# The output projection in Strassen's form, two blocks of tokens at once, in a fused Fourier-mixing and SoLU kernel

## The chip, the cores and the metric

The kernel runs on one core of a Trainium2 chip. The metric is the device time of one execution in microseconds; a time below is the median of three or four executions unless it says otherwise (of seven for the kernel before where it ran beside a batch). The engines are PE (TensorE, matmuls), PEld (its weight loads), DVE (VectorE), ACT (ScalarE), POOL (GpSimd) and SP (SyncE, which here only issues DMAs; "SPq" is its queue).

## The reference

```python
def _attn_ref(x, filt_r, filt_i):                  # x: 8 x 3136 x 256, float32
    X = np.fft.rfft(x, axis=1)
    Y = X * (filt_r + 1j * filt_i)[None, :, :]
    return np.fft.irfft(Y, n=x.shape[1], axis=1)   # then seen as 25088 x 256

def _moe_ref(x, w_in, w_out, g_ln):                # w_in 256 x 1024, w_out 1024 x 256
    h = x @ w_in
    e = np.exp(h - np.max(h, axis=-1, keepdims=True))
    solu = h * (e / (np.sum(e, axis=-1, keepdims=True) + 1e-09))
    mu = np.mean(solu, axis=-1, keepdims=True)
    var = np.mean((solu - mu) ** 2, axis=-1, keepdims=True)
    return (solu - mu) / np.sqrt(var + 1e-06) * g_ln @ w_out
```

## The kernel before

The 25088 tokens are 196 blocks of 128. The main loop has one `step` per block, 196 steps and some to drain. An even and an odd step are a pair; the hidden layer of a pair (`x @ w_in`) is already in Strassen's form, seven products instead of eight. The Fourier transforms of later batch entries are spread over the same steps as small jobs: `pa` (first stage forward), `pb` (second stage forward), `pc` (second stage back), `py` (first stage back). Their rows and tables come by DMA from SyncE's queue.

The projection takes the blocks one at a time. A block's `solu` is transposed in 32x32 pieces by VectorE, regrouped by four DMAs on SyncE's queue, and multiplied with eight chunks of `w_out`, 256 columns wide:

```python
def regroup(g, a):                       # one block a step
    turned = turns[g].rearrange("p (k q) b i -> p k q (b i)", q=4)
    solu_ts[g, a] = st = upool.tile([P, KF, P], FP32, ...)
    for q in range(4):
        nc.sync.dma_start(out=st[32 * q:32 * q + 32, :, :],
                          in_=turned[32 * a:32 * a + 32, :, q, :])
    if a == 0:                           # every fourth step: 1/sqrt(var + eps)
        ...                              # two small GpSimd instructions make rs
        for c in range(4):
            for i in range(4):           # 16 tiny copies put rs into row order
                nc.gpsimd.tensor_copy(out=rss[g][32 * i:32 * i + 32, c:c + 1],
                                      in_=rs[32 * c:32 * c + 32, i:i + 1])

def project(k, ps, half):
    ...
    for f in range(KF // 2 * half, KF // 2 * half + KF // 2):
        nc.tensor.matmul(out=ps, lhsT=solu_ts[divmod(k, 4)][:, f, :], rhs=w_out_sb[:, f, :],
                         start=(f == 0), stop=(f == KF - 1), skip_group_check=True)
```

Row buffers and lead of the loads (every x piece and every row piece of the way back passes through the pool "r"):

```python
for name, bufs in (("r", 4), ("t1", 2), ("t2", 3), ("p", 2), ("g", 2))
...
at = max(t - 3, row_loads[n - 4][0] if n >= 4 else -1)   # step at which a row load is issued
ahead(t, 3).append(lambda sp=sp, i=i: sp.fetch(i))       # t2: spectrum rows, three steps ahead
ahead(t, 2).append(lambda sp=sp, i=i: sp.fetch_de(i))    # de: their table, two steps ahead
```

Of the kernel before, what the change touches and what calls it, by code (L numbers as in the profile page):

```python
# [17 lines left out]
P = 128  # L18
# [14 lines left out]
LAG = 8  # L33
# [47 lines left out]
def kernel(  # L81
# [32 lines left out]

    w_in_sb = consts.tile([P, 7, DFF // 2], FP32, name="w_in_sb")
    w_out_sb = consts.tile([P, KF, C], FP32, name="w_out_sb")
    g_sb = consts.tile([P, KF], FP32, name="g_sb")
    neg_half = consts.tile([P, 4], FP32, name="neg_half")
    ones = consts.tile([P, P], FP32, name="ones")
    w_bar = consts.tile([P, C], FP32, name="w_bar")  # L120
# [3 lines left out]
    y = consts.tile([P, KD, PAIR], FP32, name="y")  # L124

# [19 lines left out]
    class Spectrum:  # L145
# [24 lines left out]
        def first(self, i, halves, ps, evac):  # L170

            if 0 in halves:
                self.t1s[i] = self.pools["t1"].tile([NK, NCH, C], FP32, name=f"t1_{self.n}_{i}",
                                                    tag="t1")
            for j, u in enumerate(halves):
                nc.tensor.matmul(out=ps[0:NK, j], lhsT=wf_t, rhs=self.xs[i][0:NR, 2 * u:2 * u + 2, :],  # L176
                                 start=True, stop=True)
            n0, n = 2 * halves[0], 2 * len(halves)
            evac(out=self.t1s[i][:, n0:n0 + n, :].rearrange("p n c -> p (n c)"),  # L179
                 in_=ps[0:NK].rearrange("p a b -> p (a b)"))  # L180

        def store_first(self, i, dmas):
            b, ch = divmod(i, NH // NCH)
            by_16(dmas, d1[self.n][b].rearrange("s (a n) c -> (s a) n c", a=4)[
                :, NCH * ch:NCH * ch + NCH, :], self.t1s.pop(i))
            del self.xs[i]
# [22 lines left out]
        def multiply(self, i):  # L209
# [5 lines left out]
            turned = self.pools["p"].tile([P, 2, C], FP32, name=f"i_{self.n}_{i}", tag="i")[:, 0:cols, :]  # L215
# [50 lines left out]
    with ExitStack() as st:  # L266
# [53 lines left out]
        for h in range(4):  # L320
            weights.append((w_out_sb[:, 2 * h:2 * h + 2, :].rearrange("p k d -> p (k d)"),
                            w_out_words[256 * h:256 * h + 256].rearrange("(k p) d w -> p k d w", p=P)))
# [13 lines left out]
        for i in range(2 * NH // NCH):  # L336
# [3 lines left out]
            sp.store_first(i, (nc.scalar.dma_start, nc.gpsimd.dma_start))  # L340
# [5 lines left out]
        w11, w21, w22, wt1, wt2, wt3, w12 = (w_in_sb[:, i, :] for i in range(7))  # L346
        for to, a, b in ((wt1, w12, w11), (wt3, w22, w12), (wt2, w22, wt1), (w12, w21, wt2)):
            nc.vector.tensor_tensor(out=to, in0=a, in1=b, op=ALU.subtract)
# [34 lines left out]
    def prepare_w_out(step):  # L383


        if step == 0:
            nc.vector.memset(ones, 1.0)
            for f in range(KF):
                nc.vector.tensor_scalar(out=w_out_sb[:, f, :], in0=w_out_sb[:, f, :],
                                        scalar1=g_sb[:, f:f + 1], scalar2=-float(DFF), op0=ALU.mult,  # L390
                                        op1=ALU.mult)
        elif step == 1:
            ps = psum("o", "ps_mean")[:, 0, :]
            for f in range(KF):
                nc.tensor.matmul(out=ps, lhsT=ones, rhs=w_out_sb[:, f, :],
                                 start=(f == 0), stop=(f == KF - 1))
            nc.scalar.mul(w_bar, ps, 1.0 / DFF)
        else:
            for f in range(KF):
                nc.vector.tensor_tensor(out=w_out_sb[:, f, :], in0=w_out_sb[:, f, :], in1=w_bar,  # L400
                                        op=ALU.subtract)


    ps_b = pool("ps_b", 1, PSUM)
    ps_o = pool("ps_o", 2, PSUM)
    ps_m = pool("ps_m", 1, PSUM)

# [304 lines left out]
```

## Time and profile before

| | before |
|---|---|
| median, range | 1795.54 us, 1795.15 to 1799.84 (3 runs) |
| PE busy | 96% of the span |
| first main-loop matmul | at 176.3 us |
| last pair of blocks begins | 49.2 us before the end |
| mean granted clock | 0.988 |

Two things are added here. The first is the view by stretches of time; the columns after the bounds are the length of the stretch, busy time of PE, PEld, DVE, ACT and POOL, then the granted PE clock, the DMA share and GB/s:

```profile
176.00:402.00 226.00, 206.14 (x726) 124.65 (x725) 126.89 (x266) 129.98 (x220) 113.01 (x242) 0.98 0.88 232
402.00:1746.00 1344.00, 1343.64 (x5094) 901.47 (x5093) 913.03 (x1899) 771.87 (x1272) 542.38 (x1335) 1.00 0.61 159
```

In the 1344 us of the second stretch PE has 0.4 us without work, and its clock is 1.00: it is not only busy, it runs at full speed. The second is VectorE's largest group (busy us and mean ns of one come before the second bar) and what SyncE's queue waits for (us in all, times, longest):

```profile
L512 DVE SCALAR_TENSOR_TENSOR h<-e,rsum,h 128x1024 f32<-128x1024 f32 x196 | 256.4, 1308 | 7.1 <-DMA x<-in_x_dram 0.3
```

**A measure used throughout.** I add the PE work of each pair at full clock (14 x 429 ns hidden, 6.91 us projection before and 6.22 after, 0.86 us per pa, pb and pc, 0.87 per py) and subtract it from the pair's length in the trace, start of product 1 to start of the next pair's product 1. I call the rest the **excess**. Before, the first ten pairs (steps 0 to 19) have 33.6 us of it and the other 87 intervals 7.1 us.

### The profile page before, as it was taken

Reading aid. Unit: us, or ns where it says so; the run is one execution under the profiler, and the core shown is the slowest. Engines: PE = TensorE matmul, PEld = TensorE weight load, DVE = VectorE, ACT = ScalarE, POOL = GpSimd, SP = SyncE. Lnnn points to the kernel's source line nnn. Section 1 sums busy time; section 2 is a strip of 40 time slices with the busy share of each in tenths; the row PEclk is TensorE's granted clock in tenths of the full one; section 3 lists DMA queues with packets and bytes.
Section 4 is the critical chain, followed back from the end, with each engine's and each line's share of the span. In section 5 each row is a group of like instructions: output and inputs, shape, how many; then the busy total and the mean of one; then the engine's idle time right before and its main releaser. Section 6 shows DMA issues by size and latency. Waiting matters only on the chain.

```text
span 1795.5 us, 22752 instructions
## 1 busy us (share of the span) xinstructions
PE 1721.1 (96%) x6324; PEld 1112.1 (62%) x6324; DVE 1155.9 (64%) x2370; ACT 990.9 (55%) x1623; POOL 718.8 (40%) x1698
## 2 busy tenths in 40 slices
PE   6589889999999999999999999999999999999998
PEld 2125455566666666766666666676777677666666
DVE  0794545567666665677777655667676766677773
ACT  2265555566666655566666555555655555555452
POOL 3242544465455543335445333344443332324331
PEclk9699999999999999999999999999999999999999
DMA  9786789987799765577667565567775444433334
GB/s 270 250 258 191 217 224 247 246 215 205 207 232 222 191 184 145 151 167 199 180 174 203 142 162 146 127 170 191 191 188 133 107 120 108 107 103 104 102 96 119
DMA packets 323180, 313.98 MB, mean 175 GB/s; under 512 B 26465, under 2 KB 284514, under 8 KB 323056
## 3 DMA queue, kind: packets, MB, share of 16 engines
q1 hardware_dynamic: 292496, 219.79, 48.3%
q0 software_dynamic: 28768, 86.45, 16.6%
q10 hardware_dynamic: 1792, 6.29, 1.0%
q8 instruction: 53, 0.87, 0.2%
q14 instruction: 71, 0.58, 0.1%
HBM read 131.55 MB, written 81.40 MB: 119 GB/s over the span
## 4 chain that ended last, share of the span: by engine, by line
PE 83%; DMA 9%; DVE 3%; ACT 2%; issue 1%; POOL 1%; SPq 1%; DVEq 0%; ACTq 0%; POOLq 0%
PE po L549 35%; PE m L464 30%; PE py L260 6%; PE pa L176 4%; PE pc L235 4%; PE pb L205 4%; DMA x<-in_x_dram 3%; DMA d<-t 2%; DMA t<-d 2%; DMA de<-de_tbl 1%; DVE p L226 1%; DVE p L224 1%; PE idle L370 1%; DMA solu_t<-turn 0%; DVE i L225 0%
## 5 line engine op out<-in xcount | busy, mean ns | idle before, releaser
L549 PE MATMUL po<-w_out_sb,solu_t 128*128 128x256 f32 x3136 | 724.5, 379 | 2.4 <-DMA solu_t<-turn 1.6
L549 PEld LDWEIGHTS po<-w_out_sb,solu_t 128*128 128x128 f32 x3136 | 593.3, 190 | 190.0 <-issue 114.9
L464 PE MATMUL m<-w_in_sb,sums 128*128 128x512 f32 x784 | 399.1, 600 | 7.5 <-ACT h L474 7.5
L514 ACT ACTIVATE e<-h,nmu 128x1024 f32<-128x1024 f32 x196 | 225.1, 1149 | 223.3 <-DVE h L512 219.5
L464 PE MATMUL m<-w_in_sb,y 128*128 128x512 f32 x588 | 286.8, 597 | 0.1
L474 ACT COPY h<-m 128x512 f32<-128x512 f32 x294 | 172.4, 586 | 176.6 <-PE m L464 162.9
L512 DVE SCALAR_TENSOR_TENSOR h<-e,rsum,h 128x1024 f32<-128x1024 f32 x196 | 256.4, 1308 | 7.1 <-DMA x<-in_x_dram 0.3
L488 DVE CUSTOM_DVE_ANT_0 h<-m,h 128x512 f32<-128x512 f32 x196 | 133.9, 683 | 173.3 <-ACT h L474 86.0
L243 POOL DMA_DIRECT2D d<-g x101 | 77.2, 764 | 416.0 <-ACT g L238 407.0
L522 DVE STREAM_TRANSPOSE turn<-h 128x1024 f32<-128x1024 f32 x196 | 242.2, 1236 | 0.4 <-DVE ot L558 0.3
L496 ACT ACTIVATE e<-h,nmax 128x1024 f32<-128x1024 f32 x196 | 225.8, 1152 | 0.1
L558 DVE TENSOR_SCALAR ot<-po,rs_t 128x256 f32<-128x256 f32 x196 | 94.3, 481 | 171.6 <-issue 84.9
L464 PEld LDWEIGHTS m<-w_in_sb,sums 128*128 128x128 f32 x784 | 141.3, 190 | 96.0 <-issue 72.6
L541 POOL COPY rs_t<-rs 32x1 f32<-32x1 f32 x784 | 181.6, 232 | 35.7
L464 PEld LDWEIGHTS m<-w_in_sb,y 128*128 128x128 f32 x588 | 109.7, 191 | 112.7 <-issue 92.5
L224 DVE TENSOR_TENSOR p<-pb,f 128x512 f32<-128x512 f32 (+1 forms) x101 | 69.1, 685 | 149.9 <-ACT i L217 147.5
L176 PE MATMUL pa<-x,wf_t 98*100 98x512 f32 x256 | 138.3, 649 | 25.8 <-DMA x<-in_x_dram 21.3
L260 PEld LDWEIGHTS py<-wi_t,t 100*128 100x128 f32 x1024 | 131.7, 192 | 50.1 <-issue 31.5
L263 ACT COPY y<-py 128x392 f32<-128x392 f32 x128 | 108.2, 846 | 85.8 <-PE py L260 84.8
L179 ACT COPY t<-pa 100x512 f32<-100x512 f32 (+1 forms) x112 | 71.8, 646 | 133.5 <-PE pa L176 109.9
L260 PE MATMUL py<-wi_t,t 100*128 100x98 f32 x1024 | 132.0, 273 | 2.6 <-DMA t<-d 1.6
L205 PE MATMUL pb<-t,de 128*128 128x512 f32 (+1 forms) x250 | 108.1, 532 | 19.4 <-DMA t<-d 11.5
(65 smaller groups left out, 1441.4 us busy)
## 6 DMA issues: line engine op xcount, KB each, us to landing
solu_t<-turn SPq DMA_DIRECT2D x784, 128.0 KB
t<-d SPq DMA_DIRECT2D x99, 256.0 KB
d<-g POOLq DMA_DIRECT2D x99, 256.0 KB, 4.4
out_dram<-ot SPq DMA_DIRECT2D x196, 128.0 KB
x<-in_x_dram SPq DMA_DIRECT2D x64, 384.0 KB
t<-d SPq DMA_DIRECT2D x64, 384.0 KB
d<-t POOLq DMA_DIRECT2D x48, 384.0 KB, 5.8
f<-f_dram POOLq DMA_DIRECT2D x104, 128.0 KB, 5.7
```

Source lines behind the costliest of these rows:

```text
L176: nc.tensor.matmul(out=ps[0:NK, j], lhsT=wf_t, rhs=self.xs[i][0:NR, 2 * u:2 * u + 2, :], start=True, stop=True)
L205: nc.tensor.matmul(out=ps[:, w * j:w * j + w, :], lhsT=self.des[i][:, j, 0, :], rhs=t2[:, w * j:w * j + w, :], start=True, stop=True)
L260: nc.tensor.matmul(out=psv[:, i, :], lhsT=t4s[e, ch][:, i, cb * P:cb * P + P], rhs=wi_t, start=True, stop=True)
L464: nc.tensor.matmul(out=ms[j, bank], lhsT=lhsT, rhs=w_in_sb[:, w, :], start=m in (1, 2, 7), stop=True, skip_group_check=True)
L474: nc.scalar.copy(out=h_half(k, i), in_=ms[j, 0])
L488: nc.vector.tensor_tensor_reduce(out=h_half(k, i), in0=ms[j, bank], in1=h_half(*kept), scale=1.0, scalar=sofar, op0=ALU.add, op1=ALU.min, ...
L496: nc.scalar.activation(out=e, in_=hs[k], func=AFT.Exp, bias=nmaxs.pop(k)[:, 1:2], scale=-1.0, accum_out=esum)
L512: nc.vector.scalar_tensor_tensor(out=solu, in0=e, scalar=rsum, in1=solu, op0=ALU.mult, op1=ALU.mult, accum_out=nmu)
L514: nc.scalar.activation(out=e, in_=solu, func=AFT.Square, bias=nmu, scale=-float(DFF), accum_out=variances[g][:, i:i + 1])
L522: nc.vector.transpose(out=turns[g][:, :, i, :], in_=solus.pop(k).rearrange("p (f j) -> p f j", j=32))
L541: nc.gpsimd.tensor_copy(out=rss[g][32 * i:32 * i + 32, c:c + 1], in_=rs[32 * c:32 * c + 32, i:i + 1])
L549: nc.tensor.matmul(out=ps, lhsT=solu_ts[divmod(k, 4)][:, f, :], rhs=w_out_sb[:, f, :], start=(f == 0), stop=(f == KF - 1), skip_group_chec ...
```

## The change

Its intent: one more of the two large matrix products in Strassen's form. Two blocks of tokens and the two halves of `w_out`'s rows and columns make a 2x2 problem; seven chains of eight 128-column matmuls replace 32 of 256 columns. That costs four sums of `solu` (128x512) a pair, on GpSimd. The buffers for them come from the row buffers (4 to 3), from t2 (3 to 2) and from halved t1 tiles. GpSimd is relieved of the 16 small copies: the reciprocal roots now go through DRAM by DMAs on SyncE's queue.

```diff
-             for name, bufs in (("r", 4), ("t1", 2), ("t2", 3), ("p", 2), ("g", 2))}
+             for name, bufs in (("r", 3), ("t1", 3), ("t2", 2), ("p", 2), ("g", 2))}
...
+    def regroup(p):                                   # two blocks, in every even step
...
+        for i in range(2):
+            a = 2 * second + i
+            st = upool.tile([P, KF, P], FP32, name=f"solu_t_{p}_{i}", tag=f"solu_t{i}")
...
+            for q in range(4):
+                nc.sync.dma_start(out=st[32 * q:32 * q + 32, :, :],
+                                  in_=turned[32 * a:32 * a + 32, :, q, :])
...
+            rows = rs_dram.tile([P, 4], FP32, name=f"rows_{g}", tag="rows")
+            nc.sync.dma_start(out=rows, in_=rs)
             rss[g] = small.tile([P, 4], FP32, name=f"rs_t_{g}", tag="rs_t")
-            for c in range(4):
-                for i in range(4):
-                    nc.gpsimd.tensor_copy(out=rss[g][32 * i:32 * i + 32, c:c + 1],
-                                          in_=rs[32 * c:32 * c + 32, i:i + 1])
+            for b in range(4):
+                nc.sync.dma_start(out=rss[g][32 * b:32 * b + 32, :],
+                                  in_=rows.rearrange("(a p) b -> b p a", p=32)[b])
...
+    def project_sums(p, step):
...
+        if step == 0:
...
+            sum_of(s1, a21, a22, ALU.add)
+            sum_of(a21, a11, a21, ALU.subtract)
...
+        else:
...
+            sum_of(s2, s1, a11, ALU.subtract)
+            sum_of(s4, a12, s2, ALU.subtract)
...
+    def project(p, m):
...
+        for f in range(KF // 2):
+            nc.tensor.matmul(out=pos[p, bank], lhsT=lhs[:, f, :], rhs=w[:, f, :],
+                             start=f == 0 and m in (1, 2, 7), stop=True, skip_group_check=True)
...
-            ahead(t, 3).append(lambda sp=sp, i=i: sp.fetch(i))
+            ahead(t, 2).append(lambda sp=sp, i=i: sp.fetch(i))
```

The loads of a step's Fourier data stand at the end of the step, behind the regrouping, the roots and the output stores in SyncE's queue.

## The prediction

> **What bounds the kernel now.** I read the page's engine row and its forty slices first.
>
> ```profile
> PE 1721.1 (96%) x6324; PEld 1112.1 (62%) x6324; DVE 1155.9 (64%) x2370; ACT 990.9 (55%) x1623; POOL 718.8 (40%) x1698
> ...
> PE   6589889999999999999999999999999999999998
> ...
> DMA  9786789987799765577667565567775444433334
> ```
>
> The matrix engine (PE) is at 9 or more from slice 8 on; everything else has a quarter or more of its time free. A busy matmul engine can still be stretched by waits, so next came the waits of PE alone: from 401 to 1760 us they come to 0.3 us in all. From 176 to 401 us the longest are the two below; the rest of PE's 74 us without work lies before 176 us, in the first stage, which the change leaves alone.
>
> ```profile
> PE m L464 <- ACT h L474: 7.5, 5, 4.9
> PE pb L205 <- DMA de<-de_tbl: 4.6, 4, 2.0
> ```
>
> Then the groups, for what PE does and what one matmul costs:
>
> ```profile
> L549 PE MATMUL po<-w_out_sb,solu_t 128*128 128x256 f32 x3136 | 724.5, 379 | 2.4 <-DMA solu_t<-turn 1.6
> L464 PE MATMUL m<-w_in_sb,sums 128*128 128x512 f32 x784 | 399.1, 600 | 7.5 <-ACT h L474 7.5
> L260 PE MATMUL py<-wi_t,t 100*128 100x98 f32 x1024 | 132.0, 273 | 2.6 <-DMA t<-d 1.6
> L541 POOL COPY rs_t<-rs 32x1 f32<-32x1 f32 x784 | 181.6, 232 | 35.7
> ```
>
> The means (379, 600, 273) are latencies of overlapping instructions, so the cost must come from starts. The timeline of PE, in the quiet part and near 916 us:
>
> ```profile
> 1631.50 3.62 PE L549 MATMUL po<-w_out_sb,solu_t 128*128 128x256 f32 x16
> 1634.95 1.88 PE L464 MATMUL m<-w_in_sb,sums 128*128 128x512 f32 x4
> 1636.67 1.89 PE L549 MATMUL po<-w_out_sb,solu_t 128*128 128x256 f32 x8
> ...
> 1644.56 3.62 PE L549 MATMUL po<-w_out_sb,solu_t 128*128 128x256 f32 x16
> ```
>
> ```profile
> 916.15 1.03 PE L260 MATMUL py<-wi_t,t 100*128 100x98 f32 x8
> 917.02 1.05 PE L464 MATMUL m<-w_in_sb,sums 128*128 128x512 f32 x2
> ```
>
> Start to start: 3.45 us for 16 matmuls of 256 columns is 216 ns each; 1.72 us for 4 of 512 is 430 ns; 0.87 us for 8 of 98 is 109 ns. A pair of blocks repeats after 1644.56 - 1631.50 = 13.06 us, and that is its work: 14 x 429 ns (hidden layer, every fp32 product being two instructions) + 32 x 216 ns (projection) = 6.01 + 6.91 = 12.92. Adding the Fourier jobs (0.86 us for each pa, pb, pc; 0.87 for each py) to this I get the length of every pair from the 20th step on, within 0.2 us in nearly all and 0.4 in two. So for 88 of 98 pairs PE alone sets the time; the first ten pairs took 201 us for about 170 us of PE work, with the DMA engines 0.86 busy there.
>
> **What the Trainium skill says.** "TensorE: Matmul & The Clock Gate", section "Back-to-back issue gap", gives N/2.4 + 2.5 ns; section "LDWEIGHTS (loading the stationary operand)" gives columns/1.2, so 107 ns for 128 columns, whatever the rows. The trace has 429 and 216 ns for 512 and 256 columns: the first formula with twice the columns (429.2 and 215.8). For 98 columns that would be 84 ns. The single records show, in each chain of eight, 88, 110 and then 111 to 112 ns, and weight loads 112 ns apart: below about 130 columns the load sets the pace, 5 ns above the skill's 107. "GPSIMD Engine Reference", section "3.1 Elementwise — side-by-side cycle accounting", has 4497 ns for a two-input add of 2048 elements; the trace has a median of 457 ns for 128. A line through both gives 1.26 us for 512 (estimate). Its section "1. Specifications" says that GpSimd contends with VectorE instructions with two SBUF inputs: the trace agrees, the longest 128-element add took 1.53 us, about one 1.29 us SCALAR_TENSOR_TENSOR more.
>
> **The change part by part.**
> *Projection on PE.* Removed: 32 instructions a pair at 216 ns = 6.91 us. Added: 7 products x 4 chunks x 2 = 56 instructions of 128 columns. Streaming needs 256/2.4 + 2.5 = 109 ns, the weight load 112; the first two of a chain of eight stream (109), six follow the loads (112): 0.89 us a chain, 6.22 us a pair. So an eighth fewer multiplications become a tenth less time: 0.69 us a pair, 68 us in 98 pairs. This is all there is to win, and the 88 PE-bound pairs hold 60 us of it.
> *VectorE.* Out: 196 x 481 ns = 94 us. In: 4 x 98 pieces of 128 columns at some 0.33 us (481 less 128/0.96 ns; estimate) = 130 us. It stays near 80% of a shorter pair: quiet pair 10.3 of 12.4 us.
> *ScalarE.* 3 x 98 scaled copies of 128 columns, about 0.26 us each (586 ns at 512 columns less 384/1.2; estimate) = 78 us, to some 62%.
> *GpSimd.* Out: the 784 copies, 182 us. In: 4 x 98 sums of 512 elements, 1.26 us alone and perhaps 1.7 us beside VectorE: 490 to 670 us. It goes to 60 or 70%, up to 14 of 15.7 us in a pair with two Fourier units.
> *Order of sums.* The sums of a pair are asked for at the end of a 6 us step and used a step later (the step by odd and even halves is about 6 us each in the quiet part, 8 with Fourier jobs). The pair sums of the hidden layer now queue behind the first two on GpSimd, which wait for eight regrouping DMAs (0.65 us each on the queue; the last four only after the fourth product frees its buffer). Worked out: p4 ends 6.1 us into the even step, issues end at 9.0, land by 11.5, two sums to 14.5, the needed pair sum by 16; product 6 wants it at about 19. It holds, with some 3 us.
> *Queue of SyncE.* Every fourth step the reciprocal roots go through DRAM: one store, a wait for its landing (2 to 3 us, estimate from the 2.8 us of the page's quickest store), four small loads. The Fourier rows and tables behind them leave about 15.5 us after the step's start; they are now fetched two steps ahead (rows were three) and wanted at 18.3 us when the pair is 15.7 us. That is tight: I expect 0.5 to 2 us of PE waiting in about ten of the twenty such places, 10 us in all.
> *Fewer row buffers.* With three instead of four, loads only one step ahead go from 3 to 8, two steps ahead from 16 to 28 (of 104), nearly all before step 20. There too the half-size t1 buffers (three halves where there were two wholes) make ScalarE wait for a store in the five steps with two x pieces. I put 8 us on the first twenty steps, against 5 of the 7 us they could gain.
> *Drain.* At the end, the last pair's regrouping waits for the buffer two pairs back, then for sums: 3 us more.
> Sum: 1795.5 - 60 - 5 + 10 + 8 + 3 = 1751; rounded to 1750.
>
> **The rivals.**
> (1) *PE gains nothing because the weight load is the bound.* If a 128-column fp32 matmul with its own load took 123 ns, 56 of them would make 6.9 us, as before, and with GpSimd and the fetches on top the time would be 1800. Against it: loads 112 ns apart in 128 chains of eight, with the same 128 columns. If they overlapped fully (109 ns), 1740.
> (2) *GpSimd becomes the bound or delays product 6.* For: adds that wait a whole VectorE instruction, in-order stores in the same queue. Against: 3 us of slack at product 6 and some 2 us free in the fullest pair. If sums take 2.2 us, the Fourier pairs (about 40) lose 1 us each: 1780 to 1790.
> (3) *The fetches come late.* For: the longer SyncE queue, less lead, DMA engines at 0.84 to 0.86 until 636 us, with 31,000 more tiny packets. Against: 300 us from 1519 on have no Fourier unit and a DMA share of 0.4. If every pair before step 46 and in the two later Fourier stretches loses what it won, 1770.
> (4) *VectorE paces the Fourier pairs.* Its work there is 14.3 us, plus some 1.5 us waiting for ScalarE's turned copies: 15.8 against PE's 15.7. Worth under 5 us.
>
> **Range and chances.** The gain is capped by counting at 68 us (78 if loads hide wholly), so 1730 is nearly the floor. Losses of 10 to 20 us are likely, 40 possible, and a net loss would need two rivals at once. Predicted 1750, 8 in 10 within 1730 to 1778. The 2% line is 1759.6, inside the range: faster 0.66, within 2% 0.32, slower 0.02.
>
> **What would show it right or wrong.** Right: 5488 projection matmuls whose starts lie 111 to 112 ns apart, a quiet pair of 12.4 us where it was 13.06, GpSimd's new sums at 1.3 to 1.8 us, waits of PE on rows and tables (pb, pa, py) of 10 to 25 us in all, most before 500 us. Wrong in step one if the chain takes over 0.95 us or under 0.88. Wrong in the rest if PE waits for GpSimd at product 6 or at the summed products, if VectorE or ScalarE paces the quiet pairs, or if the first twenty steps grow by over 20 us.

## More of the kernel before

```profile
SPq L562 <- DVE ot L558: 589.1, 179, 8.5
```

SyncE's queue spends a third of the span holding a finished block's store until VectorE has made it. The loads stand behind that store in the queue, but they had lead enough: PE hardly waits for any of them after 401 us.

## The result, and the profile after

The changed kernel is correct and takes **1925.11 us** (1918.79 to 1933.53, four runs) against 1795.35 (four runs of the kernel before): ratio 1.072, 95% interval 1.0672 to 1.0768. The profiled run took 1931.8 us.

Engine row and two of the slice rows of the page, after:

```profile
PE 1724.5 (89%) x8692; PEld 1165.7 (60%) x8692; DVE 1235.1 (64%) x2586; ACT 1066.6 (55%) x1917; POOL 1091.5 (57%) x1306
...
PE   6679887888899999989989989989788999999996
...
PEclk8799888889999999999999999989989999999999
```

PE's busy time has not fallen although its work has, and its clock has digits of 7 and 8 where it had nines. The stretches say the same in numbers:

```profile
176.00:402.00 226.00, 184.92 (x713) 110.77 (x712) 109.78 (x244) 113.00 (x199) 113.34 (x161) 0.87 0.75 202
402.00:1760.00 1358.00, 1253.50 (x6733) 884.46 (x6732) 920.18 (x1935) 796.75 (x1451) 820.79 (x958) 0.97 0.58 154
```

In the long stretch PE is without work for 104 us of 1358 where it was for 0.4 of 1344, and it also runs at a granted clock of 0.97 instead of 1.00.

Yet the arithmetic of the matmuls came out. Timeline of PE in the quiet part, after (start, length of the group, line; L484 is the hidden layer, L595 the projection):

```profile
1744.74 1.02 PE L484 MATMUL m<-w_in_sb,y 128*128 128x512 f32 x2
...
1746.46 1.05 PE L595 MATMUL o<-w_out_sb,u 128*128 128x128 f32 x8
1747.35 1.06 PE L595 MATMUL o<-w_out_sb,solu_t 128*128 128x128 f32 x8
1748.24 1.88 PE L484 MATMUL m<-w_in_sb,s 128*128 128x512 f32 x4
...
1757.00 1.02 PE L484 MATMUL m<-w_in_sb,y 128*128 128x512 f32 x2
```

A chain of eight takes 0.89 us from start to start, 111 ns a matmul; the same product of the next pair comes 12.26 us later, where it was 13.06. The groups of GpSimd's sums and VectorE's largest, after:

```profile
L463 POOL TENSOR_TENSOR u<-solu_t 128x512 f32<-128x512 f32 x98 | 142.6, 1455 | 244.9 <-DMA solu_t<-turn 180.5
...
L532 DVE SCALAR_TENSOR_TENSOR h<-e,rsum,h 128x1024 f32<-128x1024 f32 x196 | 306.2, 1562 | 7.1 <-DVE rsum L529 0.3
```

The sum takes 1.46 us, inside the predicted 1.3 to 1.8. The SCALAR_TENSOR_TENSOR, which the change does not touch, went from 1308 to 1562 ns.

What PE waits for now (us in all, times, longest), and then SyncE's queue, both after:

```profile
PE pb L207 <- DMA de<-de_tbl: 78.2, 22, 8.5
PE pa L180 <- DMA x<-in_x_dram: 25.6, 13, 5.7
PE py L263 <- DMA t<-d: 22.5, 4, 12.3
```

```profile
SPq L555 <- PE o L595: 222.7, 79, 10.2
SPq L555 <- DVE turn L542: 202.0, 47, 9.0
SPq L566 <- DMA rows<-rs: 97.9, 49, 4.9
```

The wait for `de`, the table of a Fourier unit, was 4.9 us. It is the *last* load of its unit, so it stands for lateness of the queue. Of the 78.2 us, 70 are in 16 steps whose number divides by four, 4.4 us each. The queue has three holders now: L555, the regrouping, waits for the fourth product to free its buffer and for the transposes; L566, the loads of the roots, for the store before them to land, 49 times 2.0 us.

One case in full: the queue's work of step 62, which begins at 805.64 us on PE; its last two loads are for the Fourier unit of step 64, which begins at 819.69. SyncE's queue, after (start, length, line, what is issued):

```profile
806.52 8.10 SPq L555 DMA_DIRECT2D solu_t<-turn  x8
814.72 0.57 SPq L563 DMA_DIRECT2D rows<-rs  x1
816.93 1.84 SPq L566 DMA_DIRECT2D rs_t<-rows  x4
818.87 1.32 SPq L622 DMA_DIRECT2D out_dram<-ot  x2
820.49 0.38 SPq L194 DMA_DIRECT2D t<-d  x1
820.93 0.46 SPq L446 DMA_DIRECT2D de<-de_tbl  x1
```

And PE in the same time:

```profile
821.46 1.02 PE L484 MATMUL m<-w_in_sb,y 128*128 128x512 f32 x2
827.90 2.04 PE L207 MATMUL pb<-t,de 128*128 128x512 f32 x2 [5.42 <-DMA de<-de_tbl]
829.74 1.91 PE L484 MATMUL m<-w_in_sb,s 128*128 128x512 f32 x2
```

Read down the queue: the regrouping takes 8.1 us with its waits, the store of the roots ends at 815.3, the loads behind it leave 1.6 us later, then two output stores, and only then `t2` and `de`. PE wants them at 822.3 and gets them at 827.9, 6.5 us after their issue ended. Then see the two L484 lines: the same two matmuls take 1.02 us before the stop and 1.91 after it. The clock records show half clock for 6.8 us there, from 1.2 us before the stop ends; so PE works at half clock for 5.6 us, which costs half of that, 2.8. The excess of the pair that begins with step 64 is 8.5 us, about the 5.4 of wait and the 2.8.

This case is not the worst. In the 16 steps with such a wait the issue of `de` begins 14.7 to 25.5 us after the start of the step two before (median 17.9), PE wants it at a median of 20.5 us, and PE starts 5.5 to 8.3 us (median 6.5) after the issue has ended.

**Where the 136 us between the two profiled runs lie** (1931.8 against 1795.5), from the excess of each part:

| part | before | after | difference |
|---|---|---|---|
| start of the main loop | 176.3 | 181.3 | +5 |
| PE work of 92 pairs with a projection, 0.69 us less each | | | -64 |
| excess, steps 0 to 19 | 33.6 | 67.1 | +34 |
| excess, later pairs | 7.1 | 154.1 | +147 |
| start of the last pair to the end | 49.2 | 63.6 | +14 |

They sum to +136. The gain is there; losses of 200 us stand against it. Of the first row little can be made: in the other runs, which leave the first stage alone, the main loop starts between 171.3 and 182.3 us.

### The profile page after: what moved, and what is told of

Same layout as the page of the kernel before. It is cut to its first block, busy times and chain, and to the rows that moved or that the text cites. A ratio compares the mean times of both kernels' runs of the same rounds, so it can differ in the third digit from the quotient of the medians. Undisturbed runs are those within 1.5% of the kernel's fastest.

```text
span 1931.8 us, 28836 instructions
## 1 busy us (share of the span) xinstructions
PE 1724.5 (89%) x8692; PEld 1165.7 (60%) x8692; DVE 1235.1 (64%) x2586; ACT 1066.6 (55%) x1917; POOL 1091.5 (57%) x1306
## 4 chain that ended last, share of the span: by engine, by line
PE 60%; DMA 17%; DVE 9%; ACT 4%; SPq 4%; issue 4%; POOL 1%; ACTq 0%; POOLq 0%; DVEq 0%
PE o L595 23%; PE m L484 22%; DMA de<-de_tbl 8%; PE py L263 5%; PE pb L207 4%; PE pa L180 4%; DMA x<-in_x_dram 3%; DVE h L532 2%; PE pc L238 2%; SPq L555 2%; DMA d<-t 2%; DMA t<-d 2%; DVE p L227 1%; DMA solu_t<-turn 1%; DVE p L229 1%
## 5 line engine op out<-in xcount | busy, mean ns | idle before, releaser
L484 PE MATMUL m<-w_in_sb,s 128*128 128x512 f32 x784 | 412.6, 618 | 8.8 <-ACT h L494 6.3
L595 PE MATMUL o<-w_out_sb,solu_t 128*128 128x128 f32 x3136 | 402.6, 277 | 8.1 <-DVE ot L614 6.1
L595 PEld LDWEIGHTS o<-w_out_sb,u 128*128 128x128 f32 x2352 | 316.0, 196 | 155.3 <-issue 128.8
L595 PEld LDWEIGHTS o<-w_out_sb,solu_t 128*128 128x128 f32 x3136 | 382.6, 194 | 38.8 <-issue 28.6
L595 PE MATMUL o<-w_out_sb,u 128*128 128x128 f32 x2352 | 319.0, 280 | 9.5 <-ACT ot L607 9.0
L532 DVE SCALAR_TENSOR_TENSOR h<-e,rsum,h 128x1024 f32<-128x1024 f32 x196 | 306.2, 1562 | 7.1 <-DVE rsum L529 0.3
L484 PE MATMUL m<-w_in_sb,y 128*128 128x512 f32 x588 | 306.1, 604 | 5.1 <-DVE h L505 3.1
L463 POOL TENSOR_TENSOR u<-solu_t 128x512 f32<-128x512 f32 x98 | 142.6, 1455 | 244.9 <-DMA solu_t<-turn 180.5
L463 POOL TENSOR_TENSOR u<-solu_t,u 128x512 f32<-128x512 f32 x98 | 145.7, 1486 | 215.0 <-PE o L595 212.3
L614 DVE SCALAR_TENSOR_TENSOR ot<-o,rs_t,ot 128x128 f32<-128x128 f32 x294 | 101.2, 344 | 229.8 <-ACT ot L607 177.9
L508 DVE CUSTOM_DVE_ANT_0 h<-m,h 128x512 f32<-128x512 f32 x196 | 133.6, 681 | 138.5 <-ACT h L494 81.6
L207 PE MATMUL pb<-t,de 128*128 128x512 f32 (+1 forms) x250 | 120.5, 586 | 98.7 <-DMA de<-de_tbl 78.2
L484 PEld LDWEIGHTS m<-w_in_sb,s 128*128 128x128 f32 x784 | 135.6, 199 | 87.4 <-issue 71.1
```

Of the source, the lines that this page charges most:

```text
L207: nc.tensor.matmul(out=ps[:, w * j:w * j + w, :], lhsT=self.des[i][:, j, 0, :], rhs=t2[:, w * j:w * j + w, :], start=True, stop=True)
L463: nc.gpsimd.tensor_tensor(out=out, in0=in0, in1=in1, op=op)
L484: nc.tensor.matmul(out=ms[j, bank], lhsT=lhsT, rhs=w_in_sb[:, w, :], start=m in (1, 2, 7), stop=True, skip_group_check=True)
L508: nc.vector.tensor_tensor_reduce(out=h_half(k, i), in0=ms[j, bank], in1=h_half(*kept), scale=1.0, scalar=sofar, op0=ALU.add, op1=ALU.min, ...
L532: nc.vector.scalar_tensor_tensor(out=solu, in0=e, scalar=rsum, in1=solu, op0=ALU.mult, op1=ALU.mult, accum_out=nmu)
L595: nc.tensor.matmul(out=pos[p, bank], lhsT=lhs[:, f, :], rhs=w[:, f, :], start=f == 0 and m in (1, 2, 7), stop=True, skip_group_check=True)
```

## The experiments

18 kernels ran, in five batches; the kernel before ran beside each batch, with medians of 1795.69, 1793.5, 1794.1, 1795.26 and 1795.51 us. The theory at the start, A in the expectations: the queue of SyncE makes Fourier loads late, and the stops halve the clock. The rivals: GpSimd's sums as such, by their time or by slowing VectorE (B); too few buffers and too short a lead, whatever stands in the queue (C); and the roots' 31,000 tiny DMA packets as such (D). Each kernel is an edit of the changed kernel unless it says otherwise. They fall under six questions.

### Is it the queue? First four edits

**e1_roots_last**: the store and loads of the roots go to the end of the even step, behind the Fourier loads.

```diff
-            rows = rs_dram.tile(...); nc.sync.dma_start(out=rows, in_=rs)
-            for b in range(4): nc.sync.dma_start(out=rss[g][...], in_=rows...)
+            roots[g] = rs
@@ end of step
+        if not odd and 0 <= j - 3 < pairs and (j - 3) % 2 == 0:
+            turn_roots((j - 3) // 2)          # the five DMAs removed above
```

> Edit: the five DMAs that carry the reciprocal roots through DRAM are issued at the end of the even step, behind the loads and the output stores, instead of ahead of them; nothing else moves. Theory A (the loads of Fourier rows and tables stand behind this hop on SyncE's queue and land too late, and PE then runs on at half clock): the 78 us that PE waits for the table de falls below 20 us, the half-clock time after the first step from 148 to under 60 us, and the time to 1800 us (1780 to 1825). Theory B (GpSimd's new sums slow VectorE and hold up the regrouping): no change, 1915 to 1930. Theory C (two t2 buffers and a lead of two steps are too little whatever stands in front): the loads come about 4 us earlier and a third of the wait stays, 1860 to 1890. Theory D (the 31,000 tiny packets clog the DMA engines): no change.

Measured: 1869.85 us (ratio 1.0397, 1.0362 to 1.0432), 55 us less than the changed kernel: in the range of theory C, outside that of A. PE's waits for `de` fall from 78.2 to 37.0 us. The wait moved rather than went (29.6 of the 37.0 are now in steps that four does not divide), as the queue shows:

```profile
SPq L572 <- DMA rows<-rs: 268.7, 49, 8.6
```

The queue now reaches that point earlier and stands there 5.5 us each time, and the loads of the *next* step are behind it.

**e2_roots_copied**: the roots are put in order by the 16 GpSimd copies of the kernel before; nothing else changes.

```diff
-            nc.sync.dma_start(out=rows, in_=rs)
-            for b in range(4): nc.sync.dma_start(out=rss[g][...], in_=rows...)
+            for c in range(4):
+                for i in range(4):
+                    nc.gpsimd.tensor_copy(out=rss[g][32 * i:32 * i + 32, c:c + 1],
+                                          in_=rs[32 * c:32 * c + 32, i:i + 1])
```

> Edit: the hop through DRAM is taken out, the roots are turned by the sixteen small GpSimd copies of the kernel before. Theory A: like the run with the hop moved, 1785 to 1825, de wait under 20 us. Theory B: GpSimd gets 182 us more work, so slower than the changed kernel, 1930 to 1950. Theory C: 1860 to 1890. Theory D: as A, and faster than the run with the hop moved by 20 us or more, which A does not expect.

Measured: 1833.49 us (1.0218, 1.0183 to 1.0252), 92 us less. Waits for `de` are some 7 us, and half clock in the pairs 51 us instead of 140. Removing five small DMAs in 49 steps gives back the greater part of the loss, although GpSimd works more. That it is also 36 us faster than e1 is what theory D had forecast and A had not; f1 below speaks against D as the cause of these waits. It also leaves a trace of GpSimd: quiet pairs alternate between 12.26 and 13.33 us, product 6 waiting 0.8 us for the sums behind the copies.

**e3_loads_first**: the whole regrouping and the output stores go behind the Fourier loads.

```diff
-            if 0 <= j - 3 < pairs: regroup(j - 3)        # in the middle of the even step
-                store_out(p)
@@ end of the even step, after the loads
+            if proj: store_out(p)
+            if 0 <= j - 3 < pairs: regroup(j - 3)
```

> Edit: in the even step the order on SyncE is loads, output stores, regrouping, hop (instead of regrouping, hop, stores, loads). The loads of the odd step now stand behind the hop with some 4 us to spare. Theory A: stalls at steps divisible by four vanish, a few of 1 to 2 us appear at odd steps, and product 6 waits for GpSimd by up to 1 us a pair because the regrouping lands later: 1790 to 1840. Theory B: slower than the changed kernel, since the sums come later. Theory C: 1860 to 1890.

Measured: 2235.33 us (1.2429), a plain miss, by 400 us. The waits for `de` are gone, but PE waits for something else:

```profile
PE m L484 <- POOL s L463: 304.6, 88, 6.7
```

The regrouping comes later, so GpSimd's first two sums wait for it, and the hidden layer's own small sums stand behind them in GpSimd's queue; product 6 waits 3.5 us in 88 of 98 pairs. The prediction had given this place 3 us of slack. The run shows that this slack is real and short: the loads cannot simply be put first.

**e5_hop_split** (on e1): the store of the roots at the end of the even step, the four loads at the end of the odd step.

```diff
-        if not odd and ...: turn_roots((j - 3) // 2)
+        if 0 <= j - 3 < pairs and (j - 3) % 2 == 0:
+            (fetch_roots if odd else store_roots)((j - 3) // 2)
```

> Edit: the hop through DRAM stays, but in two parts: its store at the end of one step and its four loads at the end of the next, each behind that step's loads, so that nothing on SyncE's queue waits for the landing. Theory A (loads late because of what stands and waits ahead of them): de wait under 15 us, as with the copies, and no GpSimd copies, so 1805 to 1835. Theory D (the tiny packets themselves clog the DMA engines): the packets are all there, so it stays where the run with the hop moved was, 1860 or more.

Measured: 1850.69 us (1.0313, 1.0282 to 1.0345), 19 us better than e1, between the ranges of A and D; waits for `de` 23.6 us. The queue still waits 192 us in all for the store to land: it runs ahead of the engines, so a step's distance in the program is little time in the queue.

### Is it GpSimd's sums?

**e4_no_sums** (wrong result): the halves of `solu` themselves stand in for the sums.

```diff
-        ... the four sum_of of a pair ...
+        solu_sums[p] = a22, a11, a21, a12
```

> Edit, wrong result on purpose: GpSimd makes no sums for the projection, the products take the plain halves of solu. PE does the same work. Theory A: the queue of SyncE is as long as before, so the stalls at steps divisible by four stay; VectorE's multiply (1562 ns) returns to about 1300 ns; 1890 to 1925. Theory B: 1740 to 1780, as the prediction had it.

Measured: 2047.37 us (1.1386), slower still, and confounded: product 3 now reads the first block's buffer itself, so that buffer comes free later and the regrouping starts later. The queue's wait for it (L555 on PE) doubles to 447.6 us and PE's waits for `de` grow to 161.7 us. It does not answer its question. Without intent it is a second dose of a late queue, and more lateness made more loss.

**e4b_fixed_sums** (wrong): constants stand in for the sums, with the buffers used and freed as in the changed kernel.

```diff
+            fixed.append(spool.tile([P, KF // 2, P], FP32, name=n, tag=n)); nc.gpsimd.memset(fixed[-1], 0.01)
-        ... the four sum_of of a pair ...
+        solu_sums[p] = fixed[0], fixed[1], a21, fixed[2]
```

> Edit on the changed kernel, wrong result on purpose: three of the four sums of solu are fixed tiles that GpSimd fills once, the fourth is the plain half, so no buffer is held longer than in the changed kernel (in the run without sums the regrouping waited for product 3 as well). Theory A: the queue of SyncE is as in the changed kernel, de wait 50 to 90 us, 1880 to 1925; VectorE's multiply falls from 1562 to about 1310 ns. Theory B (GpSimd's sums): de wait under 20 us and 1750 to 1790.

Measured: 1899.99 us (1.0605, 1.0548 to 1.0662). All the sums together give back 25 us of 130. The SCALAR_TENSOR_TENSOR is back at 1309 ns, so it was the sums that slowed it. The trace of the changed kernel shows the same one by one: the 146 of these instructions that overlap a 128x512 sum take 1653 ns on average, the other 50 take 1297. But PE still waits 60.6 us for `de` in 15 steps that divide by four. The rival "GpSimd" is real and is not the main cause.

### Mending the queue step by step

**e6_pair_sums_first** (on e5): the hidden layer's small sums are asked of GpSimd before the sums that wait for the regrouping.

```diff
+            if hid and j + 1 < pairs: pair_sums(j + 1)
             if 0 <= j - 3 < pairs: project_sums(j - 3, 0)
...
-                if j + 1 < pairs: pair_sums(j + 1)
```

> Edit on top of the split hop: on GpSimd the pair sums of the hidden layer come before the first two sums of solu, which wait for the regrouping DMAs. If product 6 waits for GpSimd because of that order (304 us in the run with the loads first, 8 us with the copies), these waits go to nearly nothing: 5 to 15 us faster than the split hop, 1795 to 1825. If the order does not matter, the same time within 3 us.

Measured: 1834.58 us (1.0213, 1.0177 to 1.0248), 16 us better than e5; waits for these sums go from 8.0 us to none that the view shows.

**e7_stores_early** (on e6): a t1 half is stored as soon as it is made, in the steps before the ninth and, for the first half, in later steps with two x pieces.

```diff
+                twice = spread(pieces, *first_at).count(t) > 1
-                stores[t].append(... sp.store_first(i, 2 * u, nc.gpsimd.dma_start))
+                (first_of if t < LAG else early if twice and u == 0 else stores)[t].append(...)
```

> Edit on top of the pair sums first: in steps before the ninth, and in the two later steps with two x pieces, a t1 half is stored right after it is evicted instead of at the end of the step. If the three t1 halves, where four are in flight, make ScalarE and then PE wait in these steps (pairs at steps 4, 6, 10 and 14 took 44 us over their PE work with the copies, 13 before), 15 to 25 us of it go: 1775 to 1805. If it is rather the three row buffers, under 5 us go.

Measured: 1825.29 us (1.0179, 1.0121 to 1.0236), above the expected range. The pair at step 6 loses 4.2 us instead of 8.9, but those at steps 10 and 14 keep 15.2 and 12.4: there PE waits for rows that were loaded one step ahead. Its interval overlaps that of e6, so the step from e6 to e7 is shown in one pair, not in the time.

**e8_hop_in_gap** (on e7): the roots' DMAs go between the two halves of a regrouping, where the queue has to wait anyway.

```diff
             if i == 1:
+                (fetch_roots if second else store_roots)(g)
             for q in range(4): nc.sync.dma_start(out=st[...], in_=turned[...])
```

> Edit on top of the early stores: both parts of the hop are issued between the first and the last four regrouping DMAs, where SyncE waits for product 4 to free the buffer anyway, the four loads one pair later than the store. In the split hop SyncE still waited 185 us for the store's landing, since its queue runs ahead of the steps. Theory A: that wait goes below 30 us, de wait under 8 us, and the time 1800 to 1815 (1825 with the early stores). If the tiny packets matter (theory D), no change.

Measured: 1845.16 us (1.0267, 1.0226 to 1.0308). The queue's wait for the roots to land is gone, and the time is no better than e7's. A miss: that wait was no longer on the path. PE still waits 22 us for `de`.

**f1_fetch_by_act** (on the changed kernel): only the issue of `t2` and `de` moves, from SyncE's queue to ScalarE's, at the same place and with the same lead.

```diff
-            nc.sync.dma_start(out=self.t2s[i][:, 0:cols, :], in_=...)
+            (nc.sync if self.n == 0 else nc.scalar).dma_start(out=self.t2s[i][:, 0:cols, :], in_=...)
-        nc.sync.dma_start(out=de[:, 0:count], in_=...)
+        nc.scalar.dma_start(out=de[:, 0:count], in_=...)
```

> Edit on the changed kernel, nothing else: the loads of Fourier rows (t2) and tables (de) are issued on ScalarE's queue at the end of the step, not on SyncE's; lead and buffers stay two steps. If the queue order is the cause and the lead of two steps enough in itself, PE's wait for de goes from 78 to under 10 us and the time to 1820 to 1850. If the lead is too short by itself (theory C), 30 us of that wait stay and the time is 1870 or more.

Measured: 1857.23 us (1.0345, 1.03 to 1.039), 68 us less than the changed kernel. This is the cleanest edit of all: the same bytes, the same lead, the same roots, another queue. What PE waits for longest is now

```profile
PE pa L180 <- DMA x<-in_x_dram: 27.1, 10, 7.4
PE py L263 <- DMA t<-d: 26.2, 8, 13.2
PE m L484 <- POOL s L463: 15.3, 12, 3.1
```

and the waits for `de`, 78.2 us before this edit, are down to 0.2. So the lead of two steps would have done (against theory C for these loads), and the same tiny packets still run (against D as the cause of these waits); the place in SyncE's queue made the loads late. Whether the packets cost anything beside that, no run separates. The time itself is 7 us above the expected range. SyncE's queue still waits 133.6 us in all for the roots to land, and the rows for `py`, in the list above, still stand in it.

**f2_gap_and_act** (on e8): the same move of `t2` and `de`.

> The same edit on the version with pair sums first, early stores and the hop in the gap (1845 us, still 22 us of PE waits for de). If those were still queue order: de wait under 5 us and 1800 to 1825. If they were the lead: unchanged, 1835 or more.

Measured: 1824.77 us (1.0145, 1.0113 to 1.0178), 100 us less than the changed kernel. Half clock in the pairs is down from 140 to 48 us. With e7 (the same within the noise) it is the fastest *correct* kernel with the change, and it is still slower than before. Its later pairs keep 66 us of excess; the single waits for VectorE and ScalarE in this run are at most 3.8 us.

### Each part alone on the kernel before

**b1_fewer_buffers** (on the kernel before): only the buffers and the leads of the change.

```diff
-             for name, bufs in (("r", 4), ("t1", 2), ("t2", 3), ...
+             for name, bufs in (("r", 3), ("t1", 3), ("t2", 2), ...      # t1 in halves
-        at = max(t - 3, row_loads[n - 4][0] if n >= 4 else -1)
+        at = max(t - 3, row_loads[n - 3][0] if n >= 3 else -1)
-            ahead(t, 3).append(lambda sp=sp, i=i: sp.fetch(i))
+            ahead(t, 2).append(lambda sp=sp, i=i: sp.fetch(i))
```

> Edit on the kernel before: only the buffers of the change (three row buffers, three half-size t1 tiles stored one by one, two t2 buffers, Fourier rows fetched two steps ahead). If fewer buffers lose the time in the first twenty steps by themselves, 15 to 35 us slower, 1810 to 1830, all of it before 420 us; the later Fourier stretches without loss. Theory C in its strong form (lead too short everywhere): 1850 or more. If they only hurt behind the longer queue: under 8 us.

Measured: 1835.75 us (1.0229, 1.02 to 1.0259), 42 us more than before. Of the excess, 62.0 us are in the first twenty steps (33.6 before) and 16.5 later (7.1). The pair at step 14 alone loses 21 us, with a wait of 9.5 us for x and 20 us at half clock. The pairs that lose most, at steps 6, 10 and 14, are those in which a row piece now has a lead of one step (steps 6, 11 and 14). Nothing of the projection's new form is in this kernel.

**b2_hop_before** (on the kernel before): only the roots through DRAM, with its buffers and its projection.

```diff
+            nc.sync.dma_start(out=rows, in_=rs)
+            for b in range(4): nc.sync.dma_start(out=rss[g][...], in_=rows...)
-            ... the 16 tensor_copy ...
```

> Edit on the kernel before: only the hop, where it stands in the change (behind the regrouping DMAs of the first block of four). Theory A: there the queue has four regrouping DMAs a step, the rows a lead of three steps, and room for 4.5 us, so under 10 us slower; PE waits for de by 2 to 10 us. If the hop by itself costs what moving it gained (55 to 90 us), 1850 or more.

Measured: 1827.63 us (1.0194, 1.0155 to 1.0233), 33 us more. I had expected it to be hidden there by the larger lead; it was not.

```profile
PE pb L205 <- DMA de<-de_tbl: 13.6, 10, 4.9
PE py L260 <- DMA t<-d: 11.6, 3, 6.2
```

Waits for `de` come from 4.9 us to 13.6, and rows for `py` from 1.6 to 11.6: the same waits as in the changed kernel, in miniature.

### How much of it is the half clock?

**e10_kept_warm**: five matmuls that nobody reads are put before the Fourier jobs in the steps that divide by four and have a unit, to keep PE busy while it would wait.

```diff
+        if k % 4 == 0 and k in warm:
+            for n in range(5):
+                nc.tensor.matmul(out=psum("b", f"warm_{k}_{n}")..., lhsT=w_in_sb[:, 0, 0:P], rhs=w_in_sb[:, 1, :], ...)
```

> Edit on the changed kernel: five needless 512-column products (ten instructions, 4.3 us at full clock) before the forward transform in each step divisible by four that has one, so that PE works instead of standing while the table comes. It adds some 17 x 4.3 = 73 us of PE work. If half of the loss is the half clock[...], the half-clock time after the first step falls from 148 to under 90 us and the kernel gets faster despite the added work: 1885 to 1912. If only the stop itself counts: 1920 to 1940.

Measured: 1967.98 us (1.0968), 43 us slower than the changed kernel, outside both expected ranges. Half clock after the first step fell from 148 to 94 us and the waits for `de` in these steps from 70 to 11, but the filler stands in 20 steps, 200 instructions or 86 us of PE work. The rest of the loss thus fell by some 43 us; as the filler replaces waits and half clock at once, this run does not say which share was the clock's. The trace of the changed kernel does: its later pairs spend 85 us at half clock, PE is at work in 61 of them, and this costs half of that, 31 of 154 us of excess, a fifth. Half clock followed every one of the 13 stops of 3.2 us or more in these pairs, and one of the three between 2.5 and 2.8. The clock lengthens a stop, it does not make one.

### Do the parts account for the whole?

**f4_fixed_on_act** (wrong): f2 with constants instead of the four sums, as in e4b.

> Wrong result on purpose: fixed tiles in place of three of the four sums of solu, on the version with the gap and ScalarE's queue. What GpSimd's sums cost once the queue is mended: VectorE's multiply back to 1310 ns from 1490, PE waits for VectorE (9 to 15 us in the Fourier stretches) mostly gone. 15 to 30 us faster than that version if they count; under 5 us if they do not.

Measured: 1794.37 us (0.9994, 0.9979 to 1.001), 30 us less than f2. VectorE's group in f2 and then in f4:

```profile
L532 DVE SCALAR_TENSOR_TENSOR h<-e,rsum,h 128x1024 f32<-128x1024 f32 x196 | 286.5, 1462 | 7.1 <-DVE rsum L529 0.3
```

```profile
L532 DVE SCALAR_TENSOR_TENSOR h<-e,rsum,h 128x1024 f32<-128x1024 f32 x196 | 255.8, 1305 | 7.1 <-DVE rsum L529 0.3
```

The excess of the later pairs falls from 65.8 to 33.1 us, that of the first twenty steps not at all (53.4 and 54.0). So the sums cost the later pairs some 30 us even with the queue mended.

**f5_fixed_four_rows** (wrong, on f4): the constants share one buffer, and what that frees goes to a fourth row buffer and a fourth t1 half; row loads are four rows ahead again.

```diff
-             for name, bufs in (("r", 3), ("t1", 3), ...
+             for name, bufs in (("r", 4), ("t1", 4), ...
-        at = max(t - 3, row_loads[n - 3][0] if n >= 3 else -1)
+        at = max(t - 3, row_loads[n - 4][0] if n >= 4 else -1)
-        solu_sums[p] = fixed[0], fixed[1], a21, fixed[2]
+        solu_sums[p] = fixed[0], fixed[0], a21, fixed[0]
```

> Wrong result on purpose (the first four operands of the projection are constants, as in f4_fixed_on_act); otherwise f2_gap_and_act with four row buffers, four half t1 buffers and the row loads four rows ahead of their use again. If the three losses add up (queue of SyncE, GpSimd's sums, fewer buffers), taking the last one out too must leave the predicted gain: f4's 1794 less 20 to 40 us, 1755 to 1775. PE's waits for rows (py, pa, pb on a DMA) in the first twenty steps fall from some 30 to under 12 us. If buffers cost little once the queue is mended (its loads leave earlier), the time stays at 1785 to 1795.

Measured: 1768.75 us (0.9838, 0.9805 to 0.9871), inside the expected 1755 to 1775 and 26 us below f4. The excess of the first twenty steps falls from 54.0 to 36.5 us (33.6 in the kernel before). PE's waits for rows in these steps fall from 19.0 us in f4 (14.2 for `py`, 4.8 for `pa`) to 4.7, under the expected 12; `pa`'s 19.9 and `pb`'s 13.1 us in the whole run lie before the main loop. `py`'s is now

```profile
PE py L263 <- DMA t<-d: 4.7, 1, 4.7
```

**f3_four_rows** (on f2, correct result): four row buffers by giving up one g buffer, and the fourth sum in place, a step later, behind the next pair's first two sums.

```diff
-             for name, bufs in (("r", 3), ("t1", 3), ("t2", 2), ("p", 2), ("g", 2))}
+             for name, bufs in (("r", 4), ("t1", 3), ("t2", 2), ("p", 2), ("g", 1))}
-            sum_of(s4, a12, s2, ALU.subtract)              # in the even step
+            sum_of(a11, a12, s2, ALU.subtract)             # at the end of the odd step
```

> On top of that, four row buffers again, paid for by one g buffer and by writing the fourth sum of solu over the first quarter (made one step later). In the kernel before, fewer buffers alone cost 42 us, 36 of them in the pairs of steps 4 to 16. If the row buffers are what those pairs lack here too, the time over PE work in the first twenty steps falls from 62 to under 40 us: 1775 to 1800, level with the kernel before or better. If the half-size t1 tiles are, under 8 us are won.

Measured: 1921.83 us (1.0704), 97 us worse than f2. The pair at step 10 is mended (3.9 us of excess for 14.3), but products with a summed operand now wait 66 us for GpSimd, whose fourth sum stands behind two that wait for the regrouping.

**f6_fourth_first** (on f3): the fourth sum before those two.

```diff
-            if 0 <= j - 3 < pairs: project_sums(j - 3, 0)
             if proj: project_sums(p, 2)
+            if 0 <= j - 3 < pairs: project_sums(j - 3, 0)
```

> Correct result. As f3_four_rows, but the fourth sum of a pair is asked of GpSimd before the first two sums of the pair behind it, so it doesn't queue behind their wait for the regrouping. If that queue was what f3 lost by, PE's waits for GpSimd at the summed products (65 us in f3) fall under 10 us and the time is f2's 1825 less 10 to 25 us: 1795 to 1815, the best correct kernel with the change, at best level with the kernel before. If the single g buffer is what f3 lost by (ScalarE held by the store, 35 us of waits for ot), the time stays above 1850.

Measured: 1851.18 us (1.0311, 1.029 to 1.0332), 71 us better than f3 and 26 worse than f2. The wait for GpSimd at the summed products is off the list of long waits, so the place in the queue was most of f3's loss. What remains is the other expected branch: PE waits 32.9 us for ScalarE's output copies (12.9 in f2), and the later pairs have 93.6 us of excess (65.8 in f2), while the first twenty steps improved from 53.4 to 43.9. The single g buffer is the likely holder of ScalarE; no run separates it from the fourth sum's new place, so that stays open. So does a correct kernel that is faster than before: none of these is.

## Why the prediction was wrong

**Right.** *Projection on PE*: the pace of 112 ns was worked out from the matmuls of 98 columns and came out as 111 to 112 ns; a quiet pair takes 12.26 us for the predicted 12.4, and the 64 us are in the table of parts. Rival (1), the weight load as the bound, is refuted by the same number. *GpSimd*: sums of 1.35 to 1.55 us, 57% busy, hidden-layer sums with small slack: e3 shows what happens when the slack is used up. *Place and kind of the lateness*: loads behind the roots' DMAs in steps that divide by four. The wait for the store's landing, put at 2 to 3 us, was 2.0. Rival (3), late fetches, was the one that came.

**The step that failed is "Queue of SyncE … 0.5 to 2 us of PE waiting in about ten of the twenty such places, 10 us in all".** It was the right wait at the wrong size: 4.4 us in 16 such steps, 70 us, and 78.2 us with the others. Three terms of its sum were mis-sized. First, the landing: leaving at 15.5, wanted at 18.3 and 0.5 to 2 us late means 3.3 to 4.8 us from issue to use; in the 16 steps PE starts 5.5 to 8.3 us (median 6.5) after the issue has ended. The profile of the kernel before held a hint: the filter loads `f` of 128 KB, on GpSimd's queue, took a median of 5.7 us to land. Second, the place in the queue: "about 15.5 us after the step's start" was 15.3 in the case shown (820.93 less 805.64) but a median of 17.9, and up to 25.5, in the 16 steps. In short pairs the need also comes sooner than the 18.3 us worked out for a pair of 15.7: the pair shown takes 14.05 us, and its successor wants the load at 16.7. Third, a wait was priced as its own length; the stop of 5.4 us cost 2.8 more at half clock. A likely further link is argued and not tested: a late pair delays the buffers and so the next regrouping, which the queue then waits for. The size by the runs: without the roots' DMAs in the queue (e2) 92 us come back, and by the mere change of queue (f1) 68. The 100 us of f2 hold more than this queue, since f2 also has e6's order on GpSimd and e7's early stores.

**"Fewer row buffers … 8 us"** was mis-sized likewise: 42 us alone on the kernel before (b1), 26 us in the mended kernel (f5, which gives back row and t1 buffers but not the third t2). I had counted the loads that lost lead correctly and in the right place, before step 20, but gave each little weight because most still had a step; there the DMA engines were 0.88 busy in the kernel before, and a late row stops PE long enough to halve its clock.

**"VectorE … under 5 us"** (rival 4) left out what the Trainium skill's sentence on contention ("GPSIMD Engine Reference", section "1. Specifications") implies for the *other* engine. I had used it for GpSimd's time only, and read it loosely: the longest add, 1.53 us, is 1.08 above the median, not 1.29; it began 0.07 us after a SCALAR_TENSOR_TENSOR and ended 0.31 us after it. The SCALAR_TENSOR_TENSOR became 254 ns longer, 196 times: 50 us of VectorE's time. Taking out all the sums gives back 25 to 30 us (e4b, f4); that is this slowing and the waits for the sums themselves together, and no run parts them.

**"Drain … 3 us"** was 14 us, with half clock at the end. The term named waits for the regrouping and the sums; in the trace PE waits there 9.0 us for ScalarE's output copies (`ot`) and 0.5 for a sum. No edit was made for it, so its cause is only read from the trace.

**Do these close the sum?** From the changed kernel, the steps to f2 -100 (queue above all), sums -30, buffers -26 lead to 1769 (f5), where I had predicted 1750 with 21 us of losses allowed. The remaining 19 us are within what the parts show: the last pair to the end is 60.6 us instead of 49.2, and the later pairs have 31 us of excess instead of 7. The longest wait of PE left there is one that the prediction had no term for, 19.9 us for ScalarE's output copies, 9.1 of them after the last pair's start; no run takes it away. The repairs were made one after another, so each size holds in that order; alone on the kernel before, roots and buffers cost 33 and 42. Since f4 and f5 compute no right result, they are an account of the loss, not versions to use.

The range was too narrow for a plain reason: its argument that "a net loss would need two rivals at once" took the rivals for independent. One change brought several of them at once, and the queue alone (92 us by e2) was more than the whole gain. Of the prediction's own signs of being wrong one came, the first twenty steps, which grew by 30 us (201.5 to 231.6); PE waited only 2.4 us for GpSimd at the hidden layer's products, and the quiet pairs kept their pace.

## What to carry to other kernels

A faster step on a full engine shortens the time that everything in the in-order queues has for its lead, so before such a change walk each queue in order for one step, with every entry's wait, and ask what stands ahead of the loads; a five-DMA detour that waits for its own landing cost 92 us here (33 in the kernel before), more than the whole gain. Moving the loads to another engine's queue was a small edit and gave 68 us; pushing the regrouping behind the loads cost 310. Price a stop of the matmul engine above about 3 us at its length plus half of the time that it then works at half clock (here 5.4 + 2.8 us), and price a second engine's work also by what it does to the engine that it contends with (here 254 ns on every large VectorE instruction).

## What the Trainium skill lacked or had wrong

- "DMA: Bandwidth & Descriptors", section "Anatomy of one DMA — SWDGE (gpsimd) path", gives a fixed cost of about 2.0 us, mostly completion, for DMAs issued by GpSimd. The roots' small store, issued by SyncE, is near it (49 waits for its landing, 97.9 us), but the same wait is 5.5 us on average and up to 8.6 when the queue comes to it at another time (e1), and PE could use `de` 6.5 us after its issue had ended, in a stretch with the DMA engines 0.79 busy. No page gives the time to landing behind other transfers at such a load, which is one of the terms mis-sized here.
- "TensorE: Matmul & The Clock Gate", section "Part 1: The HAM clock gate (the "warmup" mystery)", has the half clock after an idle window of about 3.4 us and agrees: two 512-column matmuls went from 1.02 to 1.91 us after a stop of 5.4 us, and one stop of 2.56 us was followed by half clock while stops of 2.65 and 2.75 us were not. Nothing is lacking there; the size here is 197 us at half clock in the span of the changed kernel, 44 in that of the kernel before.
- The same page, section "LDWEIGHTS (loading the stationary operand)": 107 ns for 128 columns; matmuls of 128 columns in fp32, each with its own load, start 111 to 112 ns apart.
- "GPSIMD Engine Reference", section "1. Specifications", names the contention with VectorE without a size (other pages of the skill say more of it). The size here: 128x512 sums on GpSimd made VectorE's two-input instruction of 128x1024 go from 1308 to 1562 ns (1309 again without the sums), and GpSimd's sums took 1.35 to 1.55 us beside it.
